# Normalising the first batch's attention by column tiles on the tensor engine, and issuing that batch's feed-forward work in a new order

## The chip, the cores and the metric

The kernel runs on one core of a Trainium2 chip. The metric is the device time of one execution in microseconds (us).

Engines are abbreviated as in the profile: PE is the tensor engine (PEld is its loading of stationary operands), DVE the vector engine, ACT the scalar engine, POOL the general engine, SP the engine that queues most transfers. "Span" is the time from the first to the last recorded instruction. It is a little shorter than the timed execution.

## The reference

Attention of 8 batches with 8 heads (S = 512 tokens, 32 state rows, D = 64 per head) feeds a feed-forward network with SiLU:

```python
scores = scale * x @ state.T          # per batch and head: 512 x 32
a      = softmax(scores)
xread  = a @ state                    # 512 x 64
sread  = softmax(scale * state @ x.T) @ x          # 32 x 64
x      = concat(xread, sread) for all heads        # 4352 rows of 512
h      = x @ w_in                     # w_in 512 x 2048
out    = silu(h) @ w_out              # w_out 2048 x 512
```

## The kernel before

Instead of computing `xread` and multiplying it by `w_in`, the kernel multiplies the state by `w_in` once per batch. This is W1, 256 rows (8 heads of 32) by 2048 columns, made in four pieces of 512 columns. Then h is W1 transposed times aT, where aT holds the normalised attention with heads and state rows on the partitions. The heads are handled in two halves `hg` of four heads, 4 x 32 = 128 partitions each.

Three kinds of matmul:

- **W1 group**: eight matmuls of 64 x 32 tiles, four column tiles side by side, for one piece of 512 columns.
- **G1** of tile `ft`: two matmuls (one per head half) that give 128 columns of h for 512 tokens; ACT applies SiLU.
- **G2** of tile `ft`: four matmuls (token tiles 0 to 3) that add 128 columns' worth to the outputs. Token tile 3 is often done later, as filler.

```python
def w1_mms(b, cols, new=bank):                     # cut
    for f, n in cols:
        for s in range(4):
            for hg in range(2):
                nc.tensor.matmul(pss[f, hg][ds(32 * s, 32), 0:n],
                    stT[ds(r, 64), b, h // 2, s % 2, :],
                    w_in_sb[ds(r, 64), h // 2, ds(f, n)],
                    tile_position=(r, 32 * s), ...)

def norm(b, hg, parts=((nc.gpsimd, 0, 4),), nr=4):   # tokens on the partitions; cut
    for c in range(0, 4, nr):
        nc.vector.tensor_reduce(rs[:, ds(c, nr)], e[:, ds(c, nr)], axis=AX, op=ADD)
    nc.vector.reciprocal(rc[:], rs[:])
    for eng, c, n in parts:
        eng.tensor_tensor(a[:, ds(c, n)], e[:, ds(c, n)],
            rc[:, ds(c, n)].to_broadcast([128, n, 4, NS]), op=MULT)
```

Batch 0 must get from the first byte to its first G1 as fast as it can, since no other batch covers it. Before the change it computes scores with tokens on the partitions, takes exp, normalises with `norm`, turns the result by eight PE transposes, and copies it to aT. Its steady part is a loop:

```python
W0 = {2: (512, 512), 6: (1024, 512), 10: (1536, 512)}   # W1 pieces of batch 0
W1_AT = {4: 0, 6: 512}                                  # W1 pieces of batch 1
LEAD0 = [2, 2, 2, 2, 2, 3, 2, 1, 3, 3, 2, 3]            # how far G1 runs ahead of G2
for ft in range(12):
    upto(min(ft + LEAD0[ft], ready))                    # issue G1 up to this tile
    if ft == 1:
        place_one_state(1, transpose_one_state(st1_n), nc.vector)
    if ft in W0:   ...                                  # W1 group, or a pair at ft 6
    elif ft in W1_AT: ...
    for tt in range(3): G2(0, tt, ft)
    for i in T3.get(ft, ()): G2(0, 3, i)                # token tile 3, late
```

So batch 0 has four entries into W1 work: three single groups (512; batch 1's 0; 1536) and one pair (1024 with batch 1's 512). Batches 1 to 7 are computed by code that the change doesn't touch.

The softmax here doesn't subtract the row's maximum and nothing guards it: scores larger than these inputs give would overflow.

Of the kernel before, what the change touches and what calls it, by code (L numbers as in the profile page):

```python
# [8 lines left out]
FP32 = mybir.dt.float32  # L9
# [12 lines left out]
NS = 32  # L22
# [20 lines left out]
def kernel(  # L43
# [36 lines left out]
    ident = pers.tile([128, 128], BF16)  # L80
    st_b = pers.tile([128, 8, 2 * D], BF16)
# [21 lines left out]
    xT = {}  # L103
# [45 lines left out]
    def load_w_in(f, n=512):  # L149
        nc.gpsimd.dma_start(w_in_sb[:, :, ds(f, n)], win_re[:, :, ds(f, n)])  # L150
# [34 lines left out]
    make_identity(nc, ident)  # L185
    load_w_in(0, 128)
# [310 lines left out]
    def g1_first():  # L497
        g = gpool.tile([128, 512], BF16, tag="g", name="g")
        gt[0] = g
        pss = []  # L500
        for i in range(2):
            ps = psH.tile([128, 512], FP32, tag="h1", name="h1")
            pss.append(ps)
        for i in range(2):
            for hg in range(2):
                nc.tensor.matmul(
                    pss[i][:, 0:256],
                    W1[0][:, hg, 0:128],
                    aT[0][:, hg, ds(2 * i, 2), :],
                    start=(hg == 0),  # L510
                    stop=(hg == 1),
                    skip_group_check=True,
                )
        for i in range(2):
            nc.scalar.activation(g[:, ds(256 * i, 256)], pss[i][:, 0:256], func=SILU, bias=0.0)

    def g1_half(k, hg):
        b, ft = divmod(k, NFT)
        if hg == 0:
            pool, tag = (psA, "a1") if k == 1 else (psH, "h1")  # L520
            h_ps[k] = pool.tile([128, 512], FP32, tag=tag, name="h1")
        nc.tensor.matmul(  # L522
            h_ps[k][:],
            W1[b][:, hg, ds(128 * ft, 128)],
            aT[b][:, hg, :, :],
            start=(hg == 0),
            stop=(hg == 1),
            skip_group_check=True,
        )

    def emit_G1(k):
        b, ft = divmod(k, NFT)
        if b < B:
            if k == 0:
                g1_first()
                return
# [69 lines left out]
    new_o = lambda sh, dt, nm: psO.tile(sh, dt, tag=o_tags.pop(), name=nm)  # L606
    keep_busy(1, psH, "h1")
    scores(0, 0)
    exps(0, 0)
    keep_busy(1, psH, "h1")  # L610
    pe_transpose_x(0, 1, 2, new_h, both)
    norm(0, 0)
    scores(0, 1, 2)
    exps(0, 1)
    norm(0, 1, ((nc.vector, 0, 4),), 2)
    w1_cols(0, [(0, 128)], (nc.scalar, nc.scalar))
    nc.scalar.activation(warm[:], busy[:, 0:1], func=SILU, bias=0.0)
    load_w_in(1024)
# [10 lines left out]
    keep_busy(3, psH, "h1")  # L629
    banks[:] = ["a2", "a3"]  # L630
    turn[0] = 0
    pss0 = w1_mms(0, [(128, 384)])
    keep_busy(2, psH, "h1")
    for c in (0, 2):
        ps_a = (psO, psA)[c // 2].tile(
            [128, 2, 128], BF16, tag=("o1", "a0")[c // 2], name="ps_at"
        )
        at_mms(ps_a, 0, 0, c, 2)
        copy(both[c // 2], aT[0][:, 0, ds(c, 2), :], ps_a[:])
    for c in (0, 2):  # L640
        ps_a = (psO, psA)[c == 0].tile(
            [128, 2, 128], BF16, tag=("o0", "a1")[c == 0], name="ps_at"
        )
        at_mms(ps_a, 0, 1, c, 2)
        copy(nc.vector, aT[0][:, 1, ds(c, 2), :], ps_a[:])
    w1_out(0, [(128, 128)], both, pss0)
    upto(1)
    w1_out(0, [(128, 256)], (nc.vector, nc.vector), pss0, 128)
    upto(2)




    turn[0] = 0
    W0 = {2: (512, 512), 6: (1024, 512), 10: (1536, 512)}
    W1_AT = {4: 0, 6: 512}
    LEAD0 = [2, 2, 2, 2, 2, 3, 2, 1, 3, 3, 2, 3]
    T3 = {1: (0, 1), 2: (2,), 3: (3,), 4: (4,), 5: (5,), 6: (6,)}
    ready = 4
    for ft in range(12):  # L660
        upto(min(ft + LEAD0[ft], ready))
        if ft == 1:
            place_one_state(1, transpose_one_state(st1_n), nc.vector)
        if ft in W0:
            pss = w1_mms(0, [W0[ft]])
            if ft in W1_AT:
                pss1 = w1_mms(1, [(W1_AT[ft], 512)], new_h)
            w1_out(0, [W0[ft]], both, pss)
            if ft in W1_AT:
                w1_out(1, [(W1_AT[ft], 512)], both, pss1)  # L670
            ready = sum(W0[ft]) // 128
        elif ft in W1_AT:
            w1_cols(1, [(W1_AT[ft], 512)], both)
        if ft == 11:
            for hg in range(2):
                cast_x(1, nc.vector, 0, 4, 4 * hg, 4)
            load_x(3)
            pe_transpose_x(1, 0, 1, engs=(nc.vector,))
            upto(16)
            nc.scalar.activation(warm[:], busy[:, 0:1], func=EXP, bias=0.0)  # L680
        for tt in range(3):
            G2(0, tt, ft)
            if ft == 7 and tt == 0:
                upto(9)
        for i in T3.get(ft, ()):
            G2(0, 3, i)
    pe_transpose_x(1, 1, 1, engs=(nc.vector,))
    G2(0, 3, 7)
    scores(1, 0, new=new_h)
    for ft in range(8, 12):  # L690
        G2(0, 3, ft)
    scores(1, 1, new=new_h)
    exps(1, 0)
# [28 lines left out]
    transpose_x(2)  # L722
    upto(NFT + 2)
# [118 lines left out]
```

## Time and profile before

| | before |
|---|---|
| timed, three runs | 213.14 us median (213.04 to 213.22) |
| the execution that the profile shows | 214.55 us, span 212.8 us |
| PE busy | 205.8 us of the span |
| first G1 / first G2 of batch 0 in that execution | 12.64 / 13.84 us |

The profiled execution was 1.3 to 1.5 us longer than the timed runs.

PE bounds the kernel: it is busy 97% of the span and makes up 94% of the chain. There are 1575 loads of stationary operands but only 1550 matmuls, and in the G2 groups 528 loads against 481 + 30 = 511 matmuls. Twenty-five matmuls have no record. A hole in PE's row is therefore not always a wait.

The timeline of the kernel before, in the ramp of batch 0 and around 17 us. Columns are start and duration in us, engine, source line, operation, operands, tile, shapes and count.

```profile
8.29 1.06 PE L252 MATMUL ps_xt<-ident,x_rows 128*128 128x128 bf16 x8
...
11.98 0.75 PE L397 MATMUL ps_at<-ident,an 128*128 128x128 bf16 x8
...
12.64 0.85 PE L506 MATMUL h<-aT,W 128*128 128x256 bf16 x4
...
13.84 0.59 PE L563 MATMUL o<-w_out_sb,g 128*128 128x512 bf16 x2
...
17.36 0.38 PE L563 MATMUL o_a<-w_out_sb,g 128*128 128x512 bf16 x1
...
17.80 0.12 PEld L522 LDWEIGHTS <-W 128*128 128x128 bf16 x2 [0.34 <-DVE W L159]
17.80 0.60 PE L522 MATMUL h<-aT,W 128*128 128x512 bf16 x2
```

Eight transposes of 128 columns took 1.06 us at 8.29 us but 0.75 at 11.98: in this execution the PE clock was slow until about 10.2 us (starts 107 ns apart until then, 56 ns after). The clock row of the page shows 9 from the first slice on, so it does not show this: in the packed trace the records of the clock begin only at 10.20 us, and the page takes the time before as full. From 17.36 (one matmul, 0.216 us of issue) to 17.80 the timeline leaves 0.22 us, ended by the DVE's copy of W.

### The profile page before, as it was taken

Reading aid. Unit: us, or ns where it says so; the run is one execution under the profiler, and the core shown is the slowest. Engines: PE = TensorE matmul, PEld = TensorE weight load, DVE = VectorE, ACT = ScalarE, POOL = GpSimd, SP = SyncE. Lnnn points to the kernel's source line nnn. Section 1 sums busy time; section 2 is a strip of 40 time slices with the busy share of each in tenths; the row PEclk is TensorE's granted clock in tenths of the full one; section 3 lists DMA queues with packets and bytes.
Section 4 is the critical chain, followed back from the end, with each engine's and each line's share of the span. In section 5 each row is a group of like instructions: output and inputs, shape, how many; then the busy total and the mean of one; then the engine's idle time right before and its main releaser. Section 6 shows DMA issues by size and latency. Waiting matters only on the chain.

```text
span 212.8 us, 3839 instructions
## 1 busy us (share of the span) xinstructions
PE 205.8 (97%) x1550; PEld 97.9 (46%) x1575; DVE 73.8 (35%) x146; ACT 139.1 (65%) x244; POOL 39.9 (19%) x62
## 2 busy tenths in 40 slices
PE   7899999999999999999999999999999999999993
PEld 2543445345444434444444444444444444466653
DVE  2672246855851137104410752143512306100011
ACT  2685667899676877699469856886775256644410
POOL 8393213702420122012200302000200000000000
PEclk9999999999999999999999999999999999999998
DMA  5999999995639567464826429114230121011112
GB/s 189 192 205 207 285 261 313 249 242 203 99 78 265 174 130 170 101 195 102 218 64 211 79 53 240 49 52 99 65 83 17 64 82 52 0 49 49 52 49 99
DMA packets 42929, 28.65 MB, mean 135 GB/s; under 512 B 28064, under 2 KB 37792, under 8 KB 42912
## 3 DMA queue, kind: packets, MB, share of 16 engines
q1 hardware_dynamic: 36720, 20.65, 36.3%
q0 software_dynamic: 5904, 7.64, 17.4%
q8 instruction: 12, 0.20, 0.4%
q10 hardware_dynamic: 288, 0.13, 0.2%
q14 instruction: 5, 0.04, 0.1%
HBM read 17.43 MB, written 8.91 MB: 124 GB/s over the span
## 4 chain that ended last, share of the span: by engine, by line
PE 94%; DMA 2%; DVE 1%; issue 1%; ACT 0%
PE o L563 50%; PE h L522 26%; PE ps_w L468 4%; PE h L543 3%; PE o_a L563 3%; DMA x_f<-in_x_dram 2%; PE o_part L585 2%; PE ps_xt L252 1%; PE ps_sr L415 1%; PE ps_busy L165 1%; PE ps_sc L305 1%; PE ps_scT L331 1%; DVE W L159 1%; PE ps_at L397 0%; ACT xT L157 0%
## 5 line engine op out<-in xcount | busy, mean ns | idle before, releaser
L563 PE MATMUL o<-w_out_sb,g 128*128 128x512 bf16 x481 | 129.5, 379 | 1.3 <-issue 0.5
L554 ACT ACTIVATE g<-h 128x512 bf16<-128x512 f32 (+1 forms) x143 | 81.3, 573 | 35.3 <-PE h L522 20.6
L563 PEld LDWEIGHTS <-g 128*128 128x128 bf16 x528 | 50.2, 98 | 58.9 <-issue 3.8
L522 PE MATMUL h<-aT,W 128*128 128x512 bf16 x247 | 73.1, 379 | 0.2
L159 DVE COPY o_sb<-o 128x512 f32<-128x512 f32 x15 | 10.4, 690 | 91.9 <-PE o L563 87.3
L522 PEld LDWEIGHTS <-W 128*128 128x128 bf16 x254 | 24.4, 98 | 30.7 <-issue 1.2
L159 DVE CAST W<-ps_w 128x512 bf16<-128x512 f32 (+2 forms) x36 | 22.3, 658 | 23.8 <-PE ps_w L468 23.8
L157 ACT ACTIVATE W<-ps_w 128x512 bf16<-128x512 f32 (+1 forms) x32 | 16.3, 562 | 10.2 <-PE ps_w L468 10.2
L159 POOL CAST x_nat<-x_f 128x512 bf16<-128x512 f32 x24 | 14.6, 648 | 33.2 <-DMA x_f<-in_x_dram 33.2
L157 ACT ACTIVATE o_sb<-o 128x512 f32<-128x512 f32 x16 | 9.5, 597 | 14.3 <-PE o L563 11.8
L361 POOL TENSOR_TENSOR an<-e,rcn 128x512 bf16<-128x512 bf16 x5 | 7.6, 1517 | 49.1 <-DVE rcn L359 49.1
L468 PE MATMUL ps_w<-w_in_sb,stT 64*32 64x512 bf16 (+2 forms) x264 | 10.2, 374 | 0.0
L543 PE MATMUL h<-xmT,w_in_sb 128*128 128x256 bf16 x64 | 9.6, 273 | 0.1
L563 PE MATMUL o_a<-w_out_sb,g 128*128 128x512 bf16 x30 | 9.4, 379 | 0.1
L543 PEld LDWEIGHTS <-w_in_sb 128*128 128x128 bf16 x64 | 6.3, 98 | 3.9
L165 PE MATMUL ps_busy<-busy 128*128 128x512 bf16 x15 | 6.8, 563 | 1.2 <-DVE warm L172 1.2
L358 DVE TENSOR_REDUCE rs<-e 128x32 f32<-128x1024 bf16 x5 | 6.1, 1210 | 2.1 <-DMA e<-eT 2.1
L345 ACT ACTIVATE eT<-ps_scT 128x512 bf16<-128x512 f32 x10 | 5.4, 594 | 1.6 <-PE ps_scT L331 1.6
L784 ACT ACT_TABLE_LOAD x5 | 6.4, 1283 | 0.1
L381 POOL TENSOR_TENSOR an<-exp_nat,rc 128x512 bf16<-128x512 bf16 x3 | 3.1, 1046 | 17.7 <-ACT eT L345 10.8
L468 PEld LDWEIGHTS <-stT 64*32 64x32 bf16 x264 | 3.2, 90 | 5.5 <-issue 4.7
L109 POOL DMA_DIRECT2D x_f<-in_x_dram x4 | 3.3, 845 | 10.2 <-DVE x_rows L159 7.9
(76 smaller groups left out, 103.7 us busy)
## 6 DMA issues: line engine op xcount, KB each, us to landing
out_dram<-o_sb SPq DMA_DIRECT2D x33, 256.0 KB, 2.4
x_f<-in_x_dram SPq DMA_DIRECT2D x4, 1024.0 KB, 5.8
x_f<-in_x_dram POOLq DMA_DIRECT2D x2, 1024.0 KB, 11.1
w_in_sb<-in_moe_w_in_dram POOLq DMA_DIRECT2D x3, 512.0 KB, 10.1
x_f<-in_x_dram SPq DMA_DIRECT2D x2, 512.0 KB, 5.2
w_out_sb<-in_moe_w_out_dram POOLq DMA_DIRECT2D x4, 256.0 KB, 11.4
w_out_sb<-in_moe_w_out_dram POOLq DMA_DIRECT2D x2, 512.0 KB, 11.2
x_f<-in_x_dram POOLq DMA_DIRECT2D x2, 512.0 KB, 13.5
```

Of the source, the lines that this page charges most:

```text
L157: nc.scalar.activation(dst, src, func=COPY, bias=0.0)
L159: eng.tensor_copy(dst, src)
L165: nc.tensor.matmul(ps[:], busy[:, 0:128], busy[:], start=True, stop=True, skip_group_check=True)
L345: nc.scalar.activation(t[:, hg], scT_ps[hg][:], func=EXP, bias=0.0, scale=SCALE)
L358: nc.vector.tensor_reduce(rs[:], e2[b][:], axis=AX, op=ADD)
L361: eng.tensor_tensor(a[:, hg], e2[b][:, hg], rc[:, hg].to_broadcast([128, 4, 4, NS]), op=MULT)
L468: nc.tensor.matmul(pss[f, hg][ds(32 * s, 32), 0:n], stT[ds(r, 64), b, h // 2, s % 2, :], w_in_sb[ds(r, 64), h // 2, ds(f, n)], start=True, ...
L522: nc.tensor.matmul(h_ps[k][:], W1[b][:, hg, ds(128 * ft, 128)], aT[b][:, hg, :, :], start=(hg == 0), stop=(hg == 1), skip_group_check=True,)
L543: nc.tensor.matmul(ps[:, 0:256], w_in_sb[:, kt, ds(128 * ft, 128)], xmT[:, :, kt].rearrange("p t n b -> p t (n b)"), start=(kt == 0), stop ...
L554: nc.scalar.activation(g[:, 0:n], ps[:, 0:n], func=SILU, bias=0.0)
L563: nc.tensor.matmul(outs[tt][:], gt[b * NFT + ft][:, ds(128 * tt, 128)], w_out_sb[:, ft, :], start=(ft == 0), stop=(ft == NFT - 1), skip_gr ...
L784: nc.scalar.activation(warm[:], busy[:, 0:1], func=SILU, bias=0.0)
```

## The change

The intent: for batch 0, never put tokens on the partitions. Scores are computed transposed (heads and states on the partitions), exponentiated, and summed per head and token by a small matmul against a 0/1 matrix. The reciprocals are spread back over the partitions by fp32 matmuls whose stationary operand is one column of reciprocals broadcast to 32 columns, against a 128 x 128 identity. The product is aT directly, with no transposes and no copies. Each head half needs 16 of these matmuls (four chunks of 128 tokens, four column tiles). Separately, the loop is replaced by an explicit order in which the W1 pieces form two pairs and one single group. The diff is condensed: lines are joined, and "..." marks cuts.

```diff
+    def first_sums(hg, ps):
+        for c in range(4):
+            nc.tensor.matmul(ps[:, ds(4 * c, 4)], eT[0][:, hg, ds(128 * c, 128)],
+                head_of_row[:], ...)
+    def first_rc(hg):
+        rc0[hg] = att.tile([128, 4, 4], FP32, ...)
+        nc.vector.reciprocal(rc0[hg]..., sums0[hg])
+    def first_spread(hg, half):
+        for c in range(2 * half, 2 * half + 2):
+            for s in range(4):
+                nc.tensor.matmul(R0[hg][ds(32 * s, 32), ds(128 * c, 128)],
+                    rc0[hg][:, c, s : s + 1].to_broadcast([128, NS]),
+                    ident_f[:], tile_position=(0, 32 * s), ...)
+    def first_norm(hg, half):            # aT = eT * R0, 256 tokens
     ...
-    scores(0, 0); exps(0, 0); norm(0, 0) ...; at_mms(...); copy(...)
+    first_scores(0); first_exp(0); ...; first_sums(0, R0[1]); first_rc(0)
+    first_scores(1); first_exp(1)
+    first_spread(0, 0); first_spread(0, 1); first_sums(1, scT_ps[0])
+    first_norm(0, 0); first_rc(1); first_norm(0, 1)
+    ...
+    for half in range(2): first_spread(1, half)
+    for half in range(2): first_norm(1, half)
+    for half in range(2): g1_tokens(half)
     ...
-    for ft in range(12): ...             # the loop shown above
+    g2s(0, 0, 1); upto(2); g2s(0, 2); upto(4); g2s(1); g2s(0, 3)
+    place_one_state(1, transpose_one_state(st1_n), nc.vector)
+    g2s(2); g2s(1, 3)
+    w0_group(512, 0)                     # pair
+    g2s(3); upto(8); g2s(4); g2s(5); (token tile 3 of 2, 3, 4)
+    w0_group(1024, 512)                  # pair
+    g2s(6); upto(12); g2s(7); g2s(8); (token tile 3 of 5, 6, 7)
+    w0_group(1536)
+    g2s(9)
+    ...
```

Later, one transfer with a transpose is added: it brings the unnormalised attention of batch 0 into the layout that the `sread` part needs, which used to exist as a by-product.

More of the change, by code (lines that the diff above doesn't have):

```diff
@@ L80 @@
     ident = pers.tile([128, 128], BF16)
+    ident_f = pers.tile([128, 128], FP32)
+    head_of_row = pers.tile([128, 4], BF16)
     st_b = pers.tile([128, 8, 2 * D], BF16)
@@ L185 @@
     make_identity(nc, ident)
+    nc.vector.memset(head_of_row[:], 0.0)
+    for i in range(4):
+        nc.vector.memset(head_of_row[ds(32 * i, 32), i : i + 1], 1.0)
+    copy(nc.vector, ident_f[:], ident[:])
     load_w_in(0, 128)
@@ L495 @@
     h_ps = {}
-    def g1_first():
-        g = gpool.tile([128, 512], BF16, tag="g", name="g")
-        gt[0] = g
-        pss = []
-        for i in range(2):
-            ps = psH.tile([128, 512], FP32, tag="h1", name="h1")
-            pss.append(ps)
-        for i in range(2):
-            for hg in range(2):
-                nc.tensor.matmul(
-                    pss[i][:, 0:256],
-                    W1[0][:, hg, 0:128],
-                    aT[0][:, hg, ds(2 * i, 2), :],
-                    start=(hg == 0),
-                    stop=(hg == 1),
+    rc0 = {}
@@ new lines, with first_scores @@
+    sums0 = {}
+    R0 = {}
+    def first_scores(hg):
+        scT_ps[hg] = psA.tile([128, 512], FP32, tag=f"a{2 + hg}", name="ps_scT")
+        for s in range(4):
+            h = HEAD_OF_SLOT[hg][s]
+            r = 64 * (h % 2)
+            nc.tensor.matmul(
+                scT_ps[hg][ds(32 * s, 32), :],
+                stT[ds(r, 64), 0, h // 2, s % 2, :],
+                xT[0][ds(r, 64), :, h // 2, :],
+                start=True,
+                stop=True,
+                tile_position=(r, 32 * s),
+                skip_group_check=True,
+            )
@@ new lines, in first_exp @@
+    def first_exp(hg):
+        nc.scalar.activation(
+            eT[0][:, hg, :], scT_ps[hg][:], func=EXP, bias=0.0, scale=SCALE
+        )
+    def first_sums(hg, ps):
+        sums0[hg] = ps[:, 0:16]
+        for c in range(4):
+            nc.tensor.matmul(
+                ps[:, ds(4 * c, 4)],
+                eT[0][:, hg, ds(128 * c, 128)],
+                head_of_row[:],
+                start=True,
+                stop=True,
+                skip_group_check=True,
+            )
+    def first_rc(hg):
+        rc0[hg] = att.tile([128, 4, 4], FP32, tag=f"rc0{hg}", name="rc0")
+        nc.vector.reciprocal(rc0[hg].rearrange("p c s -> p (c s)"), sums0[hg])
@@ L512, in g1_first @@
+    def first_spread(hg, half):
+        for c in range(2 * half, 2 * half + 2):
+            for s in range(4):
+                nc.tensor.matmul(
+                    R0[hg][ds(32 * s, 32), ds(128 * c, 128)],
+                    rc0[hg][:, c, s : s + 1].to_broadcast([128, NS]),
+                    ident_f[:],
+                    start=True,
+                    stop=True,
+                    tile_position=(0, 32 * s),
                     skip_group_check=True,
                 )
-        for i in range(2):
-            nc.scalar.activation(g[:, ds(256 * i, 256)], pss[i][:, 0:256], func=SILU, bias=0.0)
+    def first_norm(hg, half):
+        cols = ds(256 * half, 256)
+        nc.vector.tensor_tensor(
+            aT[0][:, hg, ds(2 * half, 2), :].rearrange("p c t -> p (c t)"),
+            eT[0][:, hg, cols],
+            R0[hg][:, cols],
+            op=MULT,
+        )
@@ new lines, with g1_tokens, silu_tokens @@
+    g1_ps = {}
+    def g1_tokens(half):
+        ps = bank([128, 512], FP32, "h1")
+        g1_ps[half] = ps
+        for hg in range(2):
+            nc.tensor.matmul(
+                ps[:, 0:256],
+                W1[0][:, hg, 0:128],
+                aT[0][:, hg, ds(2 * half, 2), :],
+                start=(hg == 0),
+                stop=(hg == 1),
+                skip_group_check=True,
+            )
+    def silu_tokens(half):
+        if half == 0:
+            gt[0] = gpool.tile([128, 512], BF16, tag="g", name="g")
+        nc.scalar.activation(
+            gt[0][:, ds(256 * half, 256)], g1_ps[half][:, 0:256], func=SILU, bias=0.0
+        )
@@ L519, in g1_half @@
         if hg == 0:
-            pool, tag = (psA, "a1") if k == 1 else (psH, "h1")
-            h_ps[k] = pool.tile([128, 512], FP32, tag=tag, name="h1")
+            if k == 1:
+                h_ps[k] = psA.tile([128, 512], FP32, tag="a1", name="h1")
+            else:
+                h_ps[k] = (bank if k in IN_BANKS else new_h)([128, 512], FP32, "h1")
         nc.tensor.matmul(
@@ L533, in emit_G1 @@
         if b < B:
-            if k == 0:
-                g1_first()
-                return
             g1_half(k, 0)
@@ L606 @@
     new_o = lambda sh, dt, nm: psO.tile(sh, dt, tag=o_tags.pop(), name=nm)
+    IN_BANKS = (4, 5, 8, 9)
+    eT[0] = tpool.tile([128, 2, 512], BF16, tag="eT", name="eT")
+    aT[0] = att.tile([128, 2, 4, 128], BF16, tag="aT", name="aT")
     keep_busy(1, psH, "h1")
-    scores(0, 0)
-    exps(0, 0)
-    keep_busy(1, psH, "h1")
-    pe_transpose_x(0, 1, 2, new_h, both)
-    norm(0, 0)
-    scores(0, 1, 2)
-    exps(0, 1)
-    norm(0, 1, ((nc.vector, 0, 4),), 2)
-    w1_cols(0, [(0, 128)], (nc.scalar, nc.scalar))
-    nc.scalar.activation(warm[:], busy[:, 0:1], func=SILU, bias=0.0)
+    first_scores(0)
+    first_exp(0)
+    xt_ps = []
+    for c, n, new in (
+        (0, 2, new_h),
+        (2, 1, lambda sh, dt, nm: psA.tile(sh, dt, tag="a0", name=nm)),
+        (3, 1, new_h),
+    ):
+        ps = new([128, n, 2, 128], BF16, "ps_xt")
+        xt_ps.append((c, n, ps))
+        for i in range(n):
+            for j in range(2):
+                nc.tensor.transpose(ps[:, i, j, :], x_nat[0][:, c + i, 2 + j, :], ident[:])
+    for (c, n, ps), eng in zip(xt_ps, (nc.vector, nc.vector, nc.scalar)):
+        copy(eng, xT[0][:, ds(c, n), ds(2, 2), :], ps[:])
+    o_tags = ["o0", "o1"]
+    pss0 = w1_mms(0, [(0, 128)], new_o)
+    R0[1] = psA.tile([128, 512], FP32, tag="a1", name="ps_r")
+    first_sums(0, R0[1])
+    first_rc(0)
+    first_scores(1)
+    first_exp(1)
+    nc.scalar.activation(warm[:], busy[:, 0:1], func=SILU, bias=0.0)
+    w1_out(0, [(0, 128)], (nc.vector, nc.vector), pss0)
+    R0[0] = psA.tile([128, 512], FP32, tag="a0", name="ps_r")
+    first_spread(0, 0)
+    first_spread(0, 1)
+    first_sums(1, scT_ps[0])
+    first_norm(0, 0)
+    first_rc(1)
+    first_norm(0, 1)
     load_w_in(1024)
@@ L628 @@
         ones_beside_x(i, nc.gpsimd)
-    keep_busy(3, psH, "h1")
-    banks[:] = ["a2", "a3"]
-    turn[0] = 0
-    pss0 = w1_mms(0, [(128, 384)])
-    keep_busy(2, psH, "h1")
-    for c in (0, 2):
-        ps_a = (psO, psA)[c // 2].tile(
-            [128, 2, 128], BF16, tag=("o1", "a0")[c // 2], name="ps_at"
-        )
-        at_mms(ps_a, 0, 0, c, 2)
-        copy(both[c // 2], aT[0][:, 0, ds(c, 2), :], ps_a[:])
-    for c in (0, 2):
-        ps_a = (psO, psA)[c == 0].tile(
-            [128, 2, 128], BF16, tag=("o0", "a1")[c == 0], name="ps_at"
-        )
-        at_mms(ps_a, 0, 1, c, 2)
-        copy(nc.vector, aT[0][:, 1, ds(c, 2), :], ps_a[:])
+    pss0 = w1_mms(0, [(128, 384)], new_h)
@@ L646 @@
+    for half in range(2):
+        first_spread(1, half)
+    for half in range(2):
+        first_norm(1, half)
+    banks[:] = ["a3", "a2"]
+    turn[0] = 0
+    for half in range(2):
+        g1_tokens(half)
     w1_out(0, [(128, 128)], both, pss0)
-    upto(1)
+    for half in range(2):
+        silu_tokens(half)
     w1_out(0, [(128, 256)], (nc.vector, nc.vector), pss0, 128)
-    upto(2)
-    turn[0] = 0
-    W0 = {2: (512, 512), 6: (1024, 512), 10: (1536, 512)}
-    W1_AT = {4: 0, 6: 512}
@@ L657 @@
-    LEAD0 = [2, 2, 2, 2, 2, 3, 2, 1, 3, 3, 2, 3]
-    T3 = {1: (0, 1), 2: (2,), 3: (3,), 4: (4,), 5: (5,), 6: (6,)}
-    ready = 4
-    for ft in range(12):
-        upto(min(ft + LEAD0[ft], ready))
-        if ft == 1:
-            place_one_state(1, transpose_one_state(st1_n), nc.vector)
-        if ft in W0:
-            pss = w1_mms(0, [W0[ft]])
-            if ft in W1_AT:
-                pss1 = w1_mms(1, [(W1_AT[ft], 512)], new_h)
-            w1_out(0, [W0[ft]], both, pss)
-            if ft in W1_AT:
-                w1_out(1, [(W1_AT[ft], 512)], both, pss1)
-            ready = sum(W0[ft]) // 128
-        elif ft in W1_AT:
-            w1_cols(1, [(W1_AT[ft], 512)], both)
-        if ft == 11:
-            for hg in range(2):
-                cast_x(1, nc.vector, 0, 4, 4 * hg, 4)
-            load_x(3)
+    done[0] = 1
@@ new lines, in g2s, with w0_group @@
+    def g2s(ft, *tts):
+        for tt in tts or (0, 1, 2):
+            G2(0, tt, ft)
+    def w0_group(f, f1=None):
+        pss = w1_mms(0, [(f, 512)])
+        if f1 is not None:
+            pss1 = w1_mms(1, [(f1, 512)], new_h)
+        w1_out(0, [(f, 512)], both, pss)
+        if f1 is not None:
+            w1_out(1, [(f1, 512)], both, pss1)
+    g2s(0, 0, 1)
+    upto(2)
+    g2s(0, 2)
+    upto(4)
+    g2s(1)
+    g2s(0, 3)
+    place_one_state(1, transpose_one_state(st1_n), nc.vector)
@@ L678 @@
+    g2s(2)
+    g2s(1, 3)
+    w0_group(512, 0)
+    g2s(3)
+    upto(8)
+    g2s(4)
+    g2s(5)
+    for ft in (2, 3, 4):
+        g2s(ft, 3)
+    w0_group(1024, 512)
+    g2s(6)
+    upto(12)
+    g2s(7)
+    g2s(8)
+    for ft in (5, 6, 7):
+        g2s(ft, 3)
+    w0_group(1536)
+    g2s(9)
+    for hg in range(2):
+        cast_x(1, nc.vector, 0, 4, 4 * hg, 4)
+        if hg == 0:
+            upto(14)
             pe_transpose_x(1, 0, 1, engs=(nc.vector,))
             upto(16)
-            nc.scalar.activation(warm[:], busy[:, 0:1], func=EXP, bias=0.0)
@@ L681 @@
-        for tt in range(3):
-            G2(0, tt, ft)
-            if ft == 7 and tt == 0:
-                upto(9)
-        for i in T3.get(ft, ()):
-            G2(0, 3, i)
+    load_x(3)
+    nc.scalar.activation(warm[:], busy[:, 0:1], func=EXP, bias=0.0)
+    g2s(10)
     pe_transpose_x(1, 1, 1, engs=(nc.vector,))
-    G2(0, 3, 7)
+    g2s(11)
     scores(1, 0, new=new_h)
-    for ft in range(8, 12):
-        G2(0, 3, ft)
+    g2s(8, 3)
     scores(1, 1, new=new_h)
+    for ft in (9, 10, 11):
+        g2s(ft, 3)
@@ L722 @@
     transpose_x(2)
+    e2[0] = e2pool.tile([128, 2, 4, 4, NS], BF16, tag="e2", name="e2")
+    for hg in range(2):
+        exp_nat[0, hg] = e2[0][:, hg]
+    nc.sync.dma_start_transpose(
+        e2[0].rearrange("p g c s n -> p (g c) (s n)"), eT[0].rearrange("q g t -> q (g t)")
+    )
     upto(NFT + 2)
```

## The prediction

> **What bounds it.** PE is busy 205.8 of 212.8 us (page, busy times), and the chain of waits is 94% PE. From about 13.4 us to the end PE has nearly no hole, so a change in batch 0 is worth (a) how much earlier dense work starts and (b) the PE holes it removes later. All later batches keep their instructions.
>
> **The start now** (chain of waits and timeline, 0 to 14 us): x_f lands 5.48; transposes; scores; exp; reduce 0.67, reciprocal 0.25, multiply 1.05 on POOL or 0.69 on DVE; eight PE transposes; first G1 at 12.64, G1 of tile 1 at 13.40, first G2 at 13.84. Matmuls of 128 columns start 107 ns apart until about 10.2 us and 56 ns apart later: the slow and fast clock of the Trainium skill, "TensorE: Matmul & The Clock Gate", Part 1; the trace agrees.
>
> **Removed:** natural scores, reduces (0.67 and 0.97), two multiplies, eight transposes of `an`, four aT copies, most filler matmuls.
>
> **Added:** transposed scores (four 512-column matmuls per half, after both xT copies, so about 7.7 instead of 7.38), eight 4-column sum matmuls, reciprocals of 128x16 (0.25), 32 fp32 matmuls of 128 columns, four multiplies of 128x256 out of PSUM (estimate 0.37 each, half of the 0.69 seen for 128x512). The trace has no fp32 matmul. The Trainium skill, "FP8 and Floating Point Precision", TensorE Precision Notes, gives true fp32 four passes. Estimate: 16 x 4 passes x 56 ns / 4 column tiles at once = 0.9, with overhead 1.1 us per half at the fast clock, 2 at the slow one. For bf16 the trace shows tiles at once: eight W1 matmuls start within 30 ns.
>
> **My ramp (estimate):** exp 0 ends 9.0; sums 0 9.5 to 10.1; rc 10.4; spread 0 10.5 to 11.6; exp 1 ends 11.1; sums 1, rc 12.4; spread 1 12.5 to 13.6; last multiply ends 14.0; first G1 about 13.5 instead of 12.64, first G2 about 14.3 instead of 13.84. The new chain has two serial rounds and is not shorter; G1 of tile 1 no longer fills the first SiLU. Loss 0.7 us.
>
> **Moved, a gain:** a W1 group of eight costs about 0.4 us on PE, some 0.3 of it a drain on leaving. Pairing (512 with 0, 1024 with 512) removes one of four: 0.25 us. Two holes of 0.22 us each, PE waiting for the DVE W eviction at 17.6 and 28.9, go, because three G2 of 0.216 now follow a pair that DVE starts evicting earlier. Small SiLU stalls: 0.1 to 0.2. Sum 0.9 us. Weights limit nothing: W1 groups would start about 17.4, 22.4, 27.4; their w_in pieces land 15.1, 20.2, 25.3.
>
> **Net:** -0.2 us: 212.9 us, range 211.8 to 214.8. Faster by over 2%: 0.01; within 2%: 0.95; slower: 0.04.
>
> **Signs of right or wrong:** first G1 (line of g1_tokens) 13.0 to 14.0 us; 16 fp32 matmuls taking 0.9 to 1.5 us per half; no PE wait on the DVE W eviction at groups 512 and 1536; batch 1's first G1 within 0.6 us of 38.05; from there 174.7 us as before.
>
> **What would make it wrong:** fp32 tiles not running at once (4 us per half: 217); the clock still slow until about 13.6 because filler was removed[...] (some 2 us slower); or fp32 passes cheap, G1 at 12.3 and 212.0; later order stalls on PSUM banks or SiLU (0.57 each against 0.43 per G1 when four follow in a row).

## More of the kernel before

The profile page of the kernel before: span, busy time by engine, the granted clock in 40 slices, the engines of the chain that ended last, and three groups (source line, engine, operation, operands, count, then busy time and mean ns, then idle time before them).

```profile
span 212.8 us, 3839 instructions
PE 205.8 (97%) x1550; PEld 97.9 (46%) x1575; DVE 73.8 (35%) x146; ACT 139.1 (65%) x244; POOL 39.9 (19%) x62
...
PEclk9999999999999999999999999999999999999998
...
PE 94%; DMA 2%; DVE 1%; issue 1%; ACT 0%
...
L563 PE MATMUL o<-w_out_sb,g 128*128 128x512 bf16 x481 | 129.5, 379 | 1.3 <-issue 0.5
...
L563 PEld LDWEIGHTS <-g 128*128 128x128 bf16 x528 | 50.2, 98 | 58.9 <-issue 3.8
...
L563 PE MATMUL o_a<-w_out_sb,g 128*128 128x512 bf16 x30 | 9.4, 379 | 0.1
```

## The result, and the profile after

| | before | after |
|---|---|---|
| timed, four runs each | 213.09 us (213.01 to 213.22) | 214.43 us (214.29 to 214.51) |
| ratio | | 1.0061, 95% interval 1.0044 to 1.0079 |
| span of the profiled execution | 212.8 us | 212.4 us |
| its time | 214.55 us | 214.51 us |

A ratio here is the mean time of one kernel's fast runs over that of the other's in the same rounds, so it is not quite the ratio of the medians. The 1.3 us are real: the timed runs of the two kernels do not overlap. The range of the prediction holds the result. Its sign and its centre (0.2 us faster) miss it.

The page and the timing seem to disagree: the profiled span got shorter, the time longer. Here are the same page rows of the kernel after.

```profile
span 212.4 us, 3967 instructions
PE 206.7 (97%) x1625; PEld 97.9 (46%) x1625; DVE 73.9 (35%) x152; ACT 137.7 (65%) x240; POOL 38.9 (18%) x61
```

In this trace every matmul has its record (1625 and 1625). Its ramp, from the timeline of the kernel after:

```profile
8.09 0.25 PE L530 MATMUL ps_r<-head_of_row,eT 128*128 128x4 bf16 x4
...
8.76 1.08 PE L546 MATMUL ps_r<-ident_f,rc 128*32 128x128 f32 x32
...
9.77 0.26 PE L530 MATMUL ps_scT<-head_of_row,eT 128*128 128x4 bf16 x4
...
9.98 0.42 DVE L558 TENSOR_TENSOR aT<-eT,ps_r 128x256 bf16<-128x256 bf16 x1 [1.01 <-PE ps_r L546]
10.32 0.25 DVE L541 RECIPROCAL rc<-ps_scT 128x16 f32<-128x16 f32 x1
...
10.62 1.08 PE L546 MATMUL ps_r<-ident_f,rc 128*32 128x128 f32 x32 [0.31 <-DVE rc L541]
...
11.84 0.75 DVE L558 TENSOR_TENSOR aT<-eT,ps_r 128x256 bf16<-128x256 bf16 x2 [0.99 <-PE ps_r L546]
12.32 0.60 PE L571 MATMUL h<-aT,W 128*128 128x256 bf16 x3 [0.40 <-DVE aT L558]
...
13.06 0.61 PE L632 MATMUL o<-w_out_sb,g 128*128 128x512 bf16 x2
```

The ramp is a chain of small steps that wait for each other: sums, reciprocal, spread (1.08 us), multiply, then the same again for the other half. The second sums were issued behind the first spread. Their operand (the second exp) was ready at 9.48, they started at 9.77. The second reciprocal in turn stood behind a multiply in DVE's order. Both multiplies of the second half start only when the whole second spread has ended (11.84 us).

The steady part, same view, around the three W1 entries (at 16.89, 22.13 and 27.12 us), and its end, the W1 pair of piece 1024 of batch 1 at 37.21:

```profile
16.13 0.95 DVE L161 COPY stT<-ps_st 64x64 bf16<-64x64 bf16 x4 [2.68 <-PE ps_st L212]
...
16.89 0.88 PE L474 MATMUL ps_w<-w_in_sb,stT 64*32 64x512 bf16 x16
...
17.70 0.60 PE L632 MATMUL o<-w_out_sb,g 128*128 128x512 bf16 x2
...
22.13 0.63 PE L474 MATMUL ps_w<-w_in_sb,stT 64*32 64x512 bf16 x16
22.69 0.60 PE L632 MATMUL o<-w_out_sb,g 128*128 128x512 bf16 x2
...
27.91 0.38 PE L632 MATMUL o_a<-w_out_sb,g 128*128 128x512 bf16 x1
28.35 0.82 PE L594 MATMUL h<-aT,W 128*128 128x512 bf16 x3
...
37.21 0.63 PE L474 MATMUL ps_w<-w_in_sb,stT 64*32 64x512 bf16 x16
```

The second pair occupies PE for 22.69 - 22.13 = 0.56 us, the first for 17.70 - 16.89 = 0.81. The first needs the transposed state of batch 1, which DVE copies from 16.13 to 17.08; one of its sixteen matmuls starts at 16.89, the other fifteen from 17.14 on. At 27.91 a hole of 0.22 us remains (one matmul takes 0.216 us of issue, the next starts 0.44 later), where the prediction said that it would go.

### The profile page after: what moved, and what is told of

It reads as the page before. It is cut to its first block, busy times and chain, and to the rows that moved or that the text cites. A ratio compares the mean times of both kernels' runs of the same rounds, so it can differ in the third digit from the quotient of the medians.

```text
span 212.4 us, 3967 instructions
## 1 busy us (share of the span) xinstructions
PE 206.7 (97%) x1625; PEld 97.9 (46%) x1625; DVE 73.9 (35%) x152; ACT 137.7 (65%) x240; POOL 38.9 (18%) x61
## 4 chain that ended last, share of the span: by engine, by line
PE 96%; DVE 2%; issue 0%; ACT 0%; DVEq 0%
PE o L632 51%; PE h L594 26%; PE ps_w L474 4%; PE h L612 3%; PE o_a L632 3%; PE ps_busy L167 2%; PE o_part L654 2%; PE ps_sr L421 1%; PE ps_r L546 1%; PE ps_scT L337 1%; DVE xT L161 1%; PE ps_xt L258 1%; PE ps_sc L311 0%; DVE aT L558 0%; PE ps_scT L512 0%; DVE W L161 0%
## 5 line engine op out<-in xcount | busy, mean ns | idle before, releaser
L632 PE MATMUL o<-w_out_sb,g 128*128 128x512 bf16 x496 | 131.7, 379 | 0.1
L159 ACT ACTIVATE W<-ps_w 128x512 bf16<-128x512 f32 (+1 forms) x30 | 15.7, 581 | 14.0 <-PE ps_w L474 14.0
L632 PE MATMUL o_a<-w_out_sb,g 128*128 128x512 bf16 x32 | 10.0, 379 | 0.0
L167 PE MATMUL ps_busy<-busy 128*128 128x512 bf16 x10 | 4.6, 603 | 1.2 <-DVE warm L174 1.2
## 6 DMA issues: line engine op xcount, KB each, us to landing
x_f<-in_x_dram POOLq DMA_DIRECT2D x2, 1024.0 KB, 10.2
```

Source lines behind the costliest of these rows:

```text
L159: nc.scalar.activation(dst, src, func=COPY, bias=0.0)
L167: nc.tensor.matmul(ps[:], busy[:, 0:128], busy[:], start=True, stop=True, skip_group_check=True)
L632: nc.tensor.matmul(outs[tt][:], gt[b * NFT + ft][:, ds(128 * tt, 128)], w_out_sb[:, ft, :], start=(ft == 0), stop=(ft == NFT - 1), skip_gr ...
```

## The experiments

Theory A: the profile of before is not typical. It fell in an execution whose PE clock rose late; a usual one is 1.4 us shorter, and the change costs about that much against it. Rival B: the span is typical, and the 1.3 us lie outside the recorded instructions. For the loss itself: theory N puts it in the new attention, theory O in the new order.

### e1: the kernel before, profiled again

No edit.

> The kernel before, unchanged, profiled once more. In its profile on hand the PE clock became fast only at 10.2 us (128-column matmuls 107 ns apart until then) and the first x_f piece landed at 5.48 us; in the profile of the changed kernel these were 6.3 and 4.74 us. That profile of before has a span of 212.8 us although the timed runs took 213.1, while the changed kernel has a span of 212.4 at 214.4. Theory A (that profile of before had an unlucky, late clock start): this time the span is about 211.2 us, the clock fast by 7 us, the first G1 at 11.5 us or earlier. Theory B (the span is right and the time outside the span differs between the two kernels): span 212.8 again with a time of 213.1.

Measured: 213.16 us (212.92 to 213.28); its profiled execution took 212.96 us with a span of 211.2. The page's row of busy times:

```profile
PE 206.0 (98%) x1575; PEld 97.0 (46%) x1575; DVE 73.8 (35%) x146; ACT 139.2 (66%) x244; POOL 39.9 (19%) x62
```

Now all 1575 matmuls have records. The timeline of e1, to be laid beside that of before and after:

```profile
7.12 0.61 PE L252 MATMUL ps_xt<-ident,x_rows 128*128 128x128 bf16 x8
...
11.09 0.72 PE L506 MATMUL h<-aT,W 128*128 128x256 bf16 x4
...
12.17 0.59 PE L563 MATMUL o<-w_out_sb,g 128*128 128x512 bf16 x2
...
15.79 0.59 PE L563 MATMUL o_a<-w_out_sb,g 128*128 128x512 bf16 x2
...
16.22 0.60 PE L522 MATMUL h<-aT,W 128*128 128x512 bf16 x2
...
35.91 0.63 PE L468 MATMUL ps_w<-w_in_sb,stT 64*32 64x512 bf16 x16
```

Theory A holds in that the profiled execution was not typical. The same eight transposes took 0.61 us instead of 1.06, because the clock was fast from 5.5 us on, and the first G2 starts at 12.17 instead of 13.84. Not all of these 1.67 us are the clock: in before the first piece of x also landed later, at 5.48 us against 5.02. Among eleven runs of the kernel before on this chip, three took 214.47 to 214.53 with spans of 212.7 to 212.8, just like the profiled one; the other eight have a median of 213.01. Of the 31 runs of before in the later sessions none took more than 213.65. No trace of those three exists, so that they too had a late clock is inferred from time and span.

The second finding: the "hole" at 17.36 in before was no hole. At the same place e1 has two matmuls (15.79, x2) and the next work 0.43 us later. The missing record had misled even the chain of waits. Before (columns: start, duration, what):

```profile
17.07 0.69 DVE W L159
...
17.80 0.39 PE h L522
```

And in e1:

```profile
2.36 7.30 DMA w_in_sb<-in_moe_w_in_dram
...
14.98 0.03 issue
15.01 0.41 PE ps_w L468 x8
...
15.95 0.43 PE o_a L563 x2
16.38 0.44 PE h L522 x2
```

With the record there, the chain passes through PE and not through the DVE copy. It also begins with a transfer of w_in (2.36 to 9.66), and the W1 group of piece 512 waits 0.10 us for its own piece, which landed at 14.96 (the group starts 0.41 us after the matmul before it; an entry without a wait takes 0.31). So in a usual execution the weights do limit something, although the prediction said that they do not.

### e2 and e3: one part of the change each

e2 takes the new order with the old attention, e3 the reverse.

```diff
 e2, against before:                    e3, against after:
-    for ft in range(12): ...           -    g2s(0, 0, 1); upto(2); ... w0_group(1536) ...
+    g2s(0, 0, 1); upto(2); ...         +    for ft in range(12): ...
```

> The attention of before, the order of G1, G2 and W1 of the change. My theory (the order gains, the new attention costs): 0.4 to 0.9 us faster than before, 212.2 to 212.7, because one tile-mode switch (0.25) and the waits on the W eviction go. Rival (the order costs, for instance by PSUM banks or a SiLU queue of four): 0.3 to 1.3 us slower than before.

> The attention of the change, the order of before. My theory: the whole loss and more is here, 1.5 to 2.2 us slower than before, 214.6 to 215.3. Rival (the order costs): within 0.4 us of before.

| | median (range) | ratio to before, interval | span, profiled |
|---|---|---|---|
| e2 | 213.29 (213.21 to 213.89) | 0.9993 (0.9963 to 1.0024) | 211.8 |
| e3 | 214.10 (214.02 to 214.45) | 1.0029 (0.9999 to 1.0059) | 211.9 |

The ratios are pulled down by the three long runs of before. Against the eight others (median 213.01), the order alone costs about 0.3 us and the attention alone about 1.1; together 1.4, and the whole change measured 1.34. That subtraction of medians sets aside three runs, so I give it as a reading. My expectation for e2, a gain of 0.4 to 0.9, missed, and so did that for e3, a loss of 1.5 to 2.2. Theory N has most of the loss, theory O a small rest. Later sessions, in which before has no such long runs, agree: e5 (new attention, new order) has a ratio of 1.0056 with an interval above 1, e7 (old attention, nearly the new order) 1.0007.

Two sums show where. From the fourth G1 matmul of tile 0 to the start of the W1 pair of piece 1024 of batch 1 all kernels do the same work. By the starts in the traces this stretch takes 24.37 us in e1, 24.30 in e3, 24.57 in after and 24.97 in e2. The new order gained nothing there. (The profiled run of e2 was its second longest: x for batch 1 landed at 27.67 us instead of 26.66 as in e1, and PE waited 0.27 us for its cast.) The ramp up to that fourth matmul takes 11.54 us in e1, 12.65 in after and 12.41 in e3, from whose timeline this line is:

```profile
12.07 0.60 PE L571 MATMUL h<-aT,W 128*128 128x256 bf16 x3 [0.40 <-DVE aT L558]
```

So with the same new attention, e3 needs 0.87 us more than e1 where after needs 1.11 more. In e3 the clock was fast from 4.5 us on, in after from 6.3: about a quarter of a microsecond of the 1.11 can belong to the execution and not to the change.

The time minus the span is 1.72 to 1.86 us in every run of every kernel with the old attention, and 2.06 to 2.18 in every run with the new one. The medians are 1.78 and 2.11, so about 0.33 us lie outside the recorded instructions: rival B has a share too.

### e4: the spread in bf16

```diff
-        rc0[hg] = att.tile([128, 4, 4], FP32, ...)
+        rc0[hg] = att.tile([128, 4, 4], BF16, ...)
-                    ident_f[:],
+                    ident[:],
```

> The changed kernel with the reciprocals and the identity of the spread in bf16 instead of fp32 (a slightly coarser result, still inside the tolerance, I expect). The 16 fp32 matmuls of a half show as 32 records that start over 0.87 us; in bf16 16 records over some 0.2 us. Theory P (the fp32 passes are the cost): 1.0 to 1.3 us faster than the changed kernel, 213.1 to 213.4. Theory S (the loss is the two serial rounds and their order, the passes of half 0 hide behind exp 1): only the passes of half 1 count, 0.5 to 0.7 us faster, 213.7 to 213.9. Also watched: time minus span, which is 2.1 us with the new attention and 1.75 with the old one; if the fp32 instructions caused that, it goes back to 1.75.

Measured: five runs from 213.31 to 215.20 us, median 213.76, and one slow one of 217.14 (before beside it 213.15); ratio 1.0038 (1.0012 to 1.0063); the result is correct. The median fits theory S, but the runs spread over both theories' ranges and beyond, so the time alone does not decide between them. From the timeline of e4:

```profile
8.51 0.41 PE L547 MATMUL ps_r<-ident,rc 128*32 128x128 bf16 x16
...
10.91 0.60 PE L572 MATMUL h<-aT,W 128*128 128x256 bf16 x3 [0.38 <-DVE aT L559]
...
11.65 0.39 PE L633 MATMUL o<-w_out_sb,g 128*128 128x512 bf16 x1
...
16.01 0.63 PE L474 MATMUL ps_w<-w_in_sb,stT 64*32 64x512 bf16 x16 [0.46 <-DMA w_in_sb<-in_moe_w_in_dram]
```

Sixteen records that together take 0.41 us stand in place of thirty-two that take 1.08: each fp32 matmul appears as two records. Starts show 218 ns per set of four fp32 column tiles, against 4 x 54 for four passes of 128 columns at the fast clock. This agrees with the Trainium skill, "FP8 and Floating Point Precision", TensorE Precision Notes. The first G2 now starts at 11.65, 1.41 us sooner than in after and 0.52 sooner than in e1. Yet the kernel is no faster than before: at 16.01 PE stands waiting for the piece of w_in that landed at 15.97, and two waits of this kind cost 0.68 us together (0.53 here and 0.14 at 21.15, by starts, against an entry without a wait; the 0.86 in e11's expectation counts the 0.09 us of each entry too). In this execution an earlier start ran into the next limit. 25 matmul records are missing from this trace as well, so the single G2 at 11.65 is one of two.

### e5: the two halves of the last spread in separate banks

```diff
+    R0[1, 1] = psO.tile([128, 512], FP32, tag="o0", name="ps_rb")
     for half in range(2):
         first_spread(1, half)
-    for half in range(2):
         first_norm(1, half)
```

> The changed kernel with the second token half of spread 1 in a PSUM bank of its own and each half's multiply issued right after its spread, so that the multiply of half 0 can start before spread half 1 ends (in the trace both multiplies wait for the whole spread, 11.70 us). Theory S: the first multiply starts 0.4 us earlier, first G2 0.3 to 0.4 us earlier, 214.0 to 214.1. Rival (the multiply is not on the path, or a matmul and DVE on neighbouring banks slow each other): 214.3 to 214.5, no change.

Measured: 214.45 us (214.15 to 214.48), ratio 1.0056 (1.0043 to 1.0068). In its profile the last multiply starts at 11.46 instead of 11.84 and the first G2 at 12.68 instead of 13.06, so the wait for the whole spread was real and worth 0.38 us of ramp. The median time did not move from that of after (measured in another session, beside a before of 213.09 against 213.15 here), which is the figure that the rival named; but the profiled run was the fastest of the five, so its ramp need not be that of the others. As a question of time, e5 is inconclusive.

### e6: the second reciprocal ahead of the multiplies

```diff
     first_sums(1, scT_ps[0])
+    first_rc(1)
     first_norm(0, 0)
-    first_rc(1)
     first_norm(0, 1)
```

> The changed kernel with one DVE instruction moved: the reciprocal of head half 1 ahead of both multiplies of head half 0, instead of between them. In the trace it starts at 10.32 us behind a multiply of 0.42 although its sums were there at about 10.03. Theory S (this chain is the path): spread 1 starts 0.25 to 0.3 us earlier, 214.1 to 214.2. Rival: 214.3 to 214.5.

Measured: 214.80 us (214.26 to 216.89), ratio 1.0087 (1.0052 to 1.0122). The expected gain did not show. From the second sums to the second spread the profile has 0.68 us instead of 0.85, as meant. But in that execution the first piece of w_in landed at 8.37 us (6.98 in after), and the W1 matmuls that need it stand ahead of the sums in PE's order: a wait of 0.42 us. In that execution the small gain was covered by the transfer; of the other runs there is no trace.

### e7: the new order with tile 1's G1 first

Built on e2.

```diff
-    g2s(0, 0, 1)
     upto(2)
+    g2s(0, 0, 1)
```

> The attention of before with the new order, but G1 of tile 1 put back in front of the first G2, as the order of before had it. In the trace of the old attention with the new order PE waits 0.42 us for the first SiLU there. If that hole is what the new order loses, 0.3 us faster than that kernel (213.25 median): 212.9 to 213.0, which is also 0.2 faster than before. Rival (pairs of W1 pieces and the waits behind them cost): 213.2 to 213.4.

Measured: 213.38 us (212.97 to 213.59), ratio 1.0007 (0.9994 to 1.0021). The wait for SiLU ahead of the first G2 (0.42 us in e2) is gone, the stretch falls from 24.97 to 24.62, and the time still equals that of before, so the expected 212.9 to 213.0 missed. Three waits remain in it: the pair behind the state copies, 0.27 us for the cast of x (which landed at 27.39 us here, 26.66 in e1), and 0.22 at piece 1536.

### e8: before plus one transposing transfer

```diff
     transpose_x(2)
+    nc.sync.dma_start_transpose(spare..., w_in_sb[:, 0, 0:1024])
```

> The kernel before with one more DMA transpose of 128x1024 into a tile that nobody reads, issued where the change issues its transpose of eT. Time minus span is 1.75 us in every run of the kernels with the old attention and 2.1 in every run with the new one, fp32 or bf16. Theory: the added transpose, the one thing that lies outside PE's start, makes the 0.35: time minus span 2.1, about 213.5. Rival: it is something else of the new attention: 1.75 and 213.15.

Measured: 213.05 us against 212.94, ratio 1.0005 (0.9991 to 1.0020). Time minus span is 1.80 to 1.86 us, against 1.74 to 1.83 for before beside it. The added transfer is not the cause of the 0.33 us outside the recorded instructions (0.35 in the expectation, from spans rounded to 0.1). The fp32 matmuls are not either, since e4 has 2.1 us as well.

### e9: the order tuned, with a slip of mine

Built on e7: the state of batch 1 placed earlier, one more G2 after piece 1536, and, unwisely, all G1 up to tile 15 ahead of the transposes of x.

```diff
     upto(4)
+    place_one_state(1, transpose_one_state(st1_n), nc.vector)
     ...
     w0_group(1536)
     g2s(9)
+    g2s(8, 3)
     for hg in range(2):
         cast_x(1, nc.vector, 0, 4, 4 * hg, 4)
         if hg == 0:
-            upto(14)
-            pe_transpose_x(1, 0, 1, engs=(nc.vector,))
             upto(16)
+            pe_transpose_x(1, 0, 1, engs=(nc.vector,))
```

> A try for a version that beats both: the attention of before, the pairs of W1 pieces, G1 of tile 1 ahead of the first G2, the state of batch 1 placed before and not during the first pair (that pair took 0.81 us on PE instead of 0.56, its second half waiting for the states), one more G2 behind the 1536 piece (PE waited 0.22 there) and G1 of tiles 14 and 15 ahead of the x transposes. By the holes seen in the traces, 0.5 us less than the 213.38 of the kernel with G1 first: 212.9, 0.25 faster than before. Rival (the landing of weights and x, not the order, sets the end of batch 0): no better than before, 213.1 to 213.4.

Measured: 214.06 us (213.76 to 214.14), ratio 1.0049 (1.0037 to 1.0061): slower by 1.1 us, not faster. The first pair did fall from 0.81 to 0.56 us (15.82 to 16.38). The timeline of e9 shows the slip:

```profile
28.33 1.08 PE L524 MATMUL h<-aT,W 128*128 128x512 bf16 x4 [0.25 <-ACT g L556]
...
30.50 0.68 DVE L159 CAST x_rows<-x_f 128x1024 bf16<-128x1024 f32 x1
...
31.24 0.62 PE L252 MATMUL ps_xt<-ident,x_rows 128*128 128x128 bf16 x8 [0.74 <-DVE x_rows L159]
```

Eight G1 matmuls in a row outran SiLU (0.25 us in this view, which counts from the modelled end of a matmul; 0.42 by starts). And the second cast of x stands in DVE's order behind the copy of the first transposes. Issuing the transposes later on PE moved that copy, hence the cast, hence the next transposes: 0.74 us in this view, 0.90 by starts.

### e10: e4, e6 and e9's order together

```diff
 e4's bf16 spread, e6's reciprocal, the W1 eviction ahead of the last multiplies, e9's order
```

> The new attention with the bf16 spread, the second reciprocal first, one W1 eviction moved ahead of the last two multiplies, and the tuned order. If the ramp were what counts, its first G2 (about 11.4 us, 0.8 earlier than before) would give a span of 210.4 and 212.5. If the weights' landing binds (w_in piece 512 at 15.0 to 16.0, 1024 at 20.0 to 21.1, 1536 at 25.2 to 26.1 in all runs so far), the span is 211.0 to 211.3 and the time 213.1 to 213.4, with PE waiting for w_in in the profile.

Measured: 214.15 us (213.86 to 214.37), ratio 1.0056 (1.0044 to 1.0068). Both ranges of its expectation missed. It has the same slip (0.7 us for the cast, 0.3 for SiLU) and 0.4 us of waits for w_in, all as the view counts them, so it tells nothing new about the new attention.

### e11: e4 without waits for late weights

```diff
-                        w_in_sb[ds(r, 64), h // 2, ds(f, n)],
+                        w_in_sb[ds(r, 64), h // 2, ds(f % 512 if b == 0 else f, n)],
-            w_out_sb[:, ft, :],
+            w_out_sb[:, ft % 4 if b == 0 else ft, :],
```

Batch 0 uses only the weights that landed first, so its result is wrong (relative error 0.60).

> Wrong on purpose: the kernel with the bf16 spread, but in batch 0 the W1 pieces 512, 1024 and 1536 and G2 of tiles 4 to 15 read the weights of the first piece and of tiles 0 to 3, which have landed long before. All loads are still made. If the landing of the weights binds the faster start, the waits of 0.86 us on w_in seen there go: 0.6 to 0.9 faster than the bf16 kernel (its lower runs were 213.3 to 214.1), 212.6 to 213.0. If not: 213.3 to 213.9.

Measured: 213.41 us; four runs within 213.39 to 213.42, two of 214.58 and 215.03; ratio 1.0042 (1.0018 to 1.0066). The expected 212.6 to 213.0 missed. The w_in waits are gone and the stretch fell from 25.05 (e4) to 24.57, but the usual time is only that of e4's best runs. So late weights are not what keeps e4 above before. What they cost e4 in a usual run is not measured well: the two ran on different chips, whose runs of before differ by 0.2 us. Laid beside e1's profiled execution (0.46 us shorter), e11 has the same ramp (11.52 us); the stretch of 24.57 makes 0.20 of the difference and the time outside the recorded instructions 0.35.

### e12: e9 without the slip

```diff
     for hg in range(2):
         cast_x(1, nc.vector, 0, 4, 4 * hg, 4)
-        if hg == 0:
-            upto(16)
-            pe_transpose_x(1, 0, 1, engs=(nc.vector,))
+    upto(14)
+    pe_transpose_x(1, 0, 1, engs=(nc.vector,))
+    upto(16)
```

> The tuned order on the old attention without the slip of the last try: there G1 of tiles 14 and 15 stood ahead of the x transposes, so two G1 waited for SiLU (0.42 us) and the cast of the second half of x stood behind a late copy in DVE's order (0.90). Now both casts stand ahead of both copies, and tiles 14 and 15 come after the first transposes as in the change. Theory (the order of batch 0 has 0.4 to 0.5 us of holes in the kernel before, and the weights allow it): from the last G1 of tile 0 to the last W1 pair of batch 1 23.9 us instead of 24.3, the time 212.4 to 212.7 where before takes 212.9 to 213.1. Rival (the landing of weights and x sets it): 212.9 to 213.3, with waits on w_in or x_f in the profile.

Measured: 212.78 us (212.40 to 213.03) against 213.07 (212.80 to 213.30); ratio 0.9980 (0.9967 to 0.9994); a little above the expected 212.4 to 212.7. From its timeline:

```profile
16.14 0.63 PE L468 MATMUL ps_w<-w_in_sb,stT 64*32 64x512 bf16 x16
...
21.14 0.62 PE L468 MATMUL ps_w<-w_in_sb,stT 64*32 64x512 bf16 x16
...
26.92 0.59 PE L565 MATMUL o_a<-w_out_sb,g 128*128 128x512 bf16 x2
27.36 1.04 PE L524 MATMUL h<-aT,W 128*128 128x512 bf16 x4
```

Both pairs are short (behind the first, the record of one G2 is missing: 25 are, in this trace), the hole after piece 1536 is filled by a second G2 (26.92, then 27.36 with no gap), and the stretch takes 23.85 us, 0.5 less than e1's. The old attention with this order beats both kernels, by 0.3 us against before, a small gain, whose interval just leaves out a ratio of 1. It shows that the planned gain of the order was there to be had, but only after two waits that the order itself had made (the first SiLU, the state copies) and the old one behind piece 1536 were taken out.

## Why the prediction was right or wrong

The result fell in the range, but only because the range was 3 us wide; the account behind it did not hold. The centre failed by 1.5 us, in the step named "Moved, a gain", with smaller parts from two others. Laid out from e1's profiled execution to after's (212.96 to 214.51, so 1.55):

| term | predicted | measured |
|---|---|---|
| ramp, to the fourth G1 of tile 0 (11.54 to 12.65) | +0.7 | +1.11 (by e3's trace +0.87) |
| order, the stretch from there (24.37 to 24.57) | -0.9 | +0.20 |
| outside the recorded instructions | not considered | +0.33 |
| rest | | -0.09 |

- **"Two holes of 0.22 us each ... go."** The first hole never existed. It was a missing matmul record, which the count on the page (1550 against 1575) would have warned of. The second was real and stayed: only three G2 stand between the group and the next G1, as before. e12 removes it with one more.
- **"Pairing ... 0.25 us."** The size is right: e1's three single groups and one pair take 1.58 us of PE, and two pairs and one single at their short lengths would take about 0.56 + 0.56 + 0.34 = 1.46 (from after's and e12's starts); with one entry gap of 0.09 less, that is 0.21. The "some 0.3 of it a drain on leaving" is mis-sized: 0.31 us pass from the start of the last W1 matmul to the next work, and 0.22 of them are that matmul's own 512 columns. But the first pair took 0.81, because I had not checked when the state of batch 1 is copied. W1 work in the stretch rose to 1.71.
- **"Small SiLU stalls: 0.1 to 0.2" as a gain.** The new order made one, 0.31 us in the stretch of after (13.06 less 12.65, less the 0.11 that a G1 matmul of 256 columns takes): with G1 of tile 1 moved behind the first G2, nothing covers the first SiLU. The prediction named that move too, but only inside its loss of 0.7 for the ramp.
- **"Weights limit nothing."** This was read from an execution that ran 1.4 us late. In e1 piece 512 holds its group up by 0.10 us; in e4, whose first G2 is the earliest of all, waits for w_in cost 0.68.
- **The ramp.** The cost of the spread was right: 0.9 to 1.5 us per half expected, 1.08 measured. "First G1 13.0 to 14.0" was wrong: 11.64 for the first matmul, 12.32 for the other three. I had put the new ramp on the late clock of the profile. The difference between the kernels, not the place, is what counts, and it was 1.11, or 0.87 by e3's trace, instead of 0.7.
- **Signs.** The wait on the W eviction at 512 is gone, that at 1536 is not. Batch 1's first G1 starts at 37.77, within 0.6 of 38.05, but this was a hit by coincidence: it compares a usual execution of after with a late one of before (about 36.5 in e1). The 174.7 us from there on were right (174.6).
- **The dangers named.** Fp32 tiles did run side by side. The clock did not stay slow for want of filler: it was fast at 6.3 us in after. "Order stalls" was the one that came true.

What stays open is the 0.33 us between span and time. It comes with the new attention, whether fp32 or bf16; it is not the added transfer alone (e8), and no run here separates the remaining candidates. The traces do not show it either: the last semaphore update in the packed traces comes 1.90 to 1.93 us after the last instruction with both attentions.

## What to carry to other kernels

Before you read waits out of a profile, check that its execution is one of the usual ones (its time against the timed runs) and that its records are complete (matmuls against weight loads); a hole of exactly one matmul's length may be a record that is missing. When work is moved earlier, look up for each operand who writes it and when, on the engine's own order: here the gain of the new order was eaten by state copies and a SiLU that had been in time for the old one. A chain of small dependent steps across three engines cost more here than I had added up, and when it was shortened (e4) the next limit was a transfer, w_in.

## What the Trainium skill lacked or had wrong

- "TensorE: Matmul & The Clock Gate", Part 1, says that the clock changes around 4 us into sustained matmul work, within half a microsecond from run to run. Here filler matmuls ran from 1.19 us on, and the fast clock began 4.4 us (e12) to 6.9 us (e5) after the start of the span in thirteen traces, in after at 6.3, and at 10.2 us in the profile of before, where PE's only holes over 0.05 us from 1.19 until then were 0.44, 0.09 and 0.20 us. The page puts the ramp's penalty under 1% of a span; the execution with the late clock was about 1.4 us of 213 longer, which agrees, but it is more than the whole change. That the profile page's row of the granted clock doesn't show it (9 in the first slices in both) stands nowhere.
- "TensorEngine Tiling (Array Packing)", Key Properties, says that a change of tiling mode drains the engine and gives no length. By starts in these traces a 64 x 32 group of 512 columns has about 0.09 us of gap on entry and, counting the 0.22 us of its last matmul, 0.31 us from the start of that matmul to the next work; one group costs about 0.34 us of PE, a pair 0.56 (22.13 to 22.69 in after).
- "FP8 and Floating Point Precision", TensorE Precision Notes, gives four passes for true fp32. It agrees, also for four 32-column tiles at once, of which it doesn't speak: 218 ns per set of four, 1.08 us for sixteen matmuls in thirty-two records, against 0.41 in bf16.
- "Perfetto Trace Analysis" says that the ends of PE instructions are modelled. It doesn't say that whole matmul records can be absent: 25 of them in six of the fourteen traces (before, e4, e5, e6, e7, e12), none in the other eight. Where a 512-column matmul is missing, a false hole of 0.22 us is left; in before the chain of waits put one down to the DVE.
- No page says that time outside the recorded instructions can depend on the kernel: 1.72 to 1.86 us with the old attention, 2.06 to 2.18 with the new one.
